# Seven to nine score places between value blocks, and a new order of GpSimd's work, in a fused attention and feed-forward kernel

## The chip, the cores and the metric

The kernel runs on one core of one Trainium2 chip. The metric is the device time of one launch in microseconds; lower is better. TensorE is called PE here as in the profile, VectorE DVE, ScalarE ACT, GpSimd POOL, and SP is the engine whose queue issues the DMAs.

## The reference

```
xn  = layernorm(A_x)                                  # 1 x 2048 x 512
q, k, v = split(xn @ wqkv)                            # 32 heads of 16
p   = softmax(q @ k.T * 16**-0.5)                     # 2048 x 2048 for every head
s   = concat(p @ v) @ wo
h   = (xn @ w_gate) * (xn @ w_up)                     # 2048 x 1792
g   = silu(h @ w_down)
out = A_x + s * g
```

Everything is float32. The projections and feed-forward products are made of three float32r products each (high by high, high by low, low by high), from operands that have been split into a high part and a rest.

## The kernel before

The sequence is cut into 4 chunks of 512 queries and 16 blocks of 128 keys, the heads into 8 groups of 4. A unit `i` is one group and one chunk of queries; there are 32 units, each of 16 *rounds*, one for each block of keys, each of 4 *places*, one for each head: 512 rounds and 2048 places in all.

At a place `expo` issues one matmul `t` (128 keys by 512 queries, line 624, PSUM banks tagged `st`, of which there are three) and ACT's exponential of it into one of 11 `e` buffers (line 626). Beside it, `score` issues a matmul `s` for a unit 21 rounds ahead (line 599, three banks tagged `s`) and DVE's maximum over it (line 601); those maxima become the offsets of the later exponentials. `t` and `s` use different 64-row halves of PE, so they run side by side. The last 21 rounds have no `s`.

Every two rounds `block` (line 629) multiplies their eight `e` tiles with the values: 8 float32 matmuls `pv` in 32-column strips, 16 records in the trace, into one more `st` bank. ACT copies the bank to `part` (line 646) and POOL adds it to the unit's sum `acc` (line 647). Late in the kernel DVE adds it from PSUM itself (line 643). The block of two rounds is issued when four more places have been issued, so twelve places are outstanding for 11 buffers, and the twelfth exponential waits for the block.

The other work of PE is the *filler*: 13 pairs of projections `p`, 56 pairs of gate and up products `g` and `u`, 24 pairs of down products `y`, then the output products `z`. `pair` (line 273) makes two products at once, one on the lower and one on the upper half of PE, in two halves of 12 slots (15 for most `y`). Between the halves ACT reads one element (`look`, line 294), and the second half waits for it. When a pair of projections or of gate and up is done, ACT copies its first product out of PSUM at once, in the place where the filler then stands. DVE's part of it (for `g` and `u` the product, line 354), with the splits on POOL that belong to it, is put in the list `before_values` and issued just before the next block.

`Filler` spreads the filler over cycles, from one block to the next. A first sum gives the number of cycles of each pair, two or three, so that 2328 slots fill 240 cycles; a pair of 24 slots in three cycles has 8, then 7 (4 of the first half and 3 of the second), then 9. In a cycle of eight places the filler stands in the six gaps that `GAPS` names, not behind the first place and not behind the last before the block.

After the 240 cycles `ending` supplies the output products `z`, in pairs of 24 slots over two cycles each, for the first three chunks of queries and, without the last four heads, for the fourth. `end` multiplies with the gate and adds the input. `finish` normalises a unit (two 32 by 32 transposes, a reciprocal and a product). After the last block `finish`, `last_heads` and `final` do this for the last unit and add its product to the fourth chunk's banks.

PE, ACT and DVE run in the order of the program. For POOL and SP that holds for the first 18 rounds only; afterwards the compiler's scheduler orders their queues.

## Time and profile before

| | us |
|---|---|
| median of 3 runs | 1743.56 (1740.57 to 1744.34) |
| the profiled execution | 1742.61 |
| its span, first to last instruction | 1740.8 |
| PE busy | 1720.9 |
| DVE busy | 1453.0 |
| ACT busy | 1324.5 |
| POOL busy | 872.3 |

The mean granted clock of PE was 0.997. In the views that follow, a row of the timeline has the start in us, the duration, engine, line, operation, tiles and count, and in brackets the engine's idle time before it with what ended it. A row of the table by stretch has the stretch, its length and each engine's busy time with its number of instructions, then the granted clock, the share of the DMA engines and GB/s. A row of the waits has the waiting instruction, the one waited for, the total in us, the number of times and the longest.

### The profile page before, as it was taken

Reading aid. Unit: us, or ns where it says so; the run is one execution under the profiler, and the core shown is the slowest. Engines: PE = TensorE matmul, PEld = TensorE weight load, DVE = VectorE, ACT = ScalarE, POOL = GpSimd, SP = SyncE. Lnnn points to the kernel's source line nnn. Section 1 sums busy time; section 2 is a strip of 40 time slices with the busy share of each in tenths; the row PEclk is TensorE's granted clock in tenths of the full one; section 3 lists DMA queues with packets and bytes.
Section 4 is the critical chain, followed back from the end, with each engine's and each line's share of the span. In section 5 each row is a group of like instructions: output and inputs, shape, how many; then the busy total and the mean of one; then the engine's idle time right before and its main releaser. Section 6 shows DMA issues by size and latency. Waiting matters only on the chain.

```text
span 1740.8 us, 35038 instructions
## 1 busy us (share of the span) xinstructions
PE 1720.9 (99%) x13574; PEld 1063.8 (61%) x13574; DVE 1453.0 (83%) x2454; ACT 1324.5 (76%) x2567; POOL 872.3 (50%) x906
## 2 busy tenths in 40 slices
PE   8999999999999999999999999999999999999998
PEld 6666566666666666666666665666666666666654
DVE  6788788888888888888888888888888888888843
ACT  6357778778777778877777888877778777777774
POOL 5225444654654547455364663653547455365450
PEclk9999999999999999999999999999999999999999
DMA  5317533611231132421015220411135121011342
GB/s 206 106 47 223 206 134 117 155 53 35 60 82 49 49 101 78 77 53 54 29 57 125 71 65 29 102 53 41 45 97 123 42 53 53 29 55 50 129 144 73
DMA packets 117234, 145.78 MB, mean 84 GB/s; under 512 B 12620, under 2 KB 74060, under 8 KB 114380
## 3 DMA queue, kind: packets, MB, share of 16 engines
q1 hardware_dynamic: 117068, 143.55, 28.1%
q8 instruction: 106, 1.74, 0.4%
q14 instruction: 60, 0.49, 0.1%
HBM read 95.94 MB, written 47.45 MB: 82 GB/s over the span
## 4 chain that ended last, share of the span: by engine, by line
PE 93%; POOL 2%; DVE 2%; DMA 1%; ACT 1%; issue 1%; SPq 0%; POOLq 0%; ACTq 0%; DVEq 0%
PE pv L637 26%; PE t L624 17%; PE s L599 13%; PE u L286 6%; PE g L286 5%; PE y L290 5%; PE y L286 4%; PE u L290 3%; PE p L286 3%; PE g L290 3%; PE v L267 2%; PE z L286 1%; PE p L290 1%; DVE mx L601 1%; PE z L290 1%
## 5 line engine op out<-in xcount | busy, mean ns | idle before, releaser
L601 DVE TENSOR_REDUCE mx<-s 128x1 f32<-128x512 f32 x2048 | 1273.5, 684 | 219.6 <-PE s L599 178.4
L626 ACT ACTIVATE e<-t 128x512 f32<-128x512 f32 x2048 | 1109.3, 603 | 248.7 <-PE pv L637 198.8
L624 PE MATMUL t<-qs,ks 50*128 50x512 f32 x2048 | 785.0, 408 | 5.5 <-ACT part L646 5.0
L599 PE MATMUL s<-ks,qs 48*128 48x512 f32 x2048 | 782.8, 416 | 0.4 <-DVE mx L601 0.4
L624 PEld LDWEIGHTS t<-qs,ks 50*128 50x128 f32 x2048 | 359.2, 185 | 286.1 <-ACT e L626 217.8
L637 PE MATMUL pv<-e,V 128*32 128x512 f32 x4096 | 492.6, 598 | 0.0
L64 POOL TENSOR_TENSOR acc<-acc,part 128x512 f32<-128x512 f32 x214 | 276.1, 1290 | 398.4 <-ACT part L646 398.0
L599 PEld LDWEIGHTS s<-ks,qs 48*128 48x128 f32 x2048 | 350.1, 184 | 29.7 <-issue 5.0
L637 PEld LDWEIGHTS pv<-e,V 128*32 128x32 f32 x4096 | 107.0, 109 | 234.0 <-issue 197.6
L646 ACT ACTIVATE part<-pv 128x512 f32<-128x512 f32 x214 | 128.2, 599 | 85.0 <-PE pv L637 74.2
L64 POOL CAST w0h<-w0r 128x512 fp32r<-128x512 f32 x60 | 36.7, 611 | 110.3 <-PE g L290 63.9
L286 PE MATMUL u<-fh,w0h 64*128 64x512 f32 x224 | 90.6, 405 | 0.0
L290 PE MATMUL g<-fh,w1h 64*128 64x512 f32 x224 | 90.4, 404 | 0.0
L290 PE MATMUL y<-dh,hh 64*128 64x512 f32 x224 | 89.5, 399 | 0.1
L286 PE MATMUL y<-dh,hh 64*128 64x512 f32 x224 | 89.3, 399 | 0.2 <-DVE y L421 0.2
L286 PE MATMUL u<-fh,w0l 64*128 64x512 f32 x224 | 88.2, 394 | 0.0
L286 PE MATMUL g<-fh,w1l 64*128 64x512 f32 x224 | 88.1, 393 | 0.0
L286 PE MATMUL y<-dl,hh 64*128 64x512 f32 x224 | 88.0, 393 | 0.0
L290 PE MATMUL g<-fl,w1h 64*128 64x512 f32 x224 | 88.0, 393 | 0.0
L290 PE MATMUL g<-fh,w1l 64*128 64x512 f32 x224 | 88.0, 393 | 0.0
L286 PE MATMUL g<-fl,w1h 64*128 64x512 f32 x224 | 88.0, 393 | 0.0
L290 PE MATMUL u<-fl,w0h 64*128 64x512 f32 x224 | 87.9, 392 | 0.0
(258 smaller groups left out, 3034.3 us busy)
## 6 DMA issues: line engine op xcount, KB each, us to landing
w1r<-in_wg_dram SPq DMA_DIRECT2D x56, 256.0 KB
w0r<-in_wu_dram SPq DMA_DIRECT2D x56, 256.0 KB
wdr<-in_wd_dram SPq DMA_DIRECT2D x56, 256.0 KB
qs<-QD SPq DMA_DIRECT2D x64, 192.0 KB
ks<-KD SPq DMA_DIRECT2D x12, 768.0 KB
KD<-hl SPq DMA_DIRECT2D x16, 512.0 KB
QD<-hl SPq DMA_DIRECT2D x16, 512.0 KB
OD<-acc SPq DMA_DIRECT2D x31, 256.0 KB
```

The lines of the kernel that those rows point to most:

```text
L64: got = getattr(self.engine, name)(*args, **kw)
L267: nc.tensor.matmul(o, l(d), r(d), start=k == d == 0, stop=k == 2 and d == ND - 1)
L286: nc.tensor.matmul(outs[k], l[LOWER], r[LOWER], start=k == 0 and n == 0, stop=(stop or k == 0) and n == len(low) - 1, skip_group_check=k == 1)
L290: nc.tensor.matmul(outs[1 - k], l[UPPER], r[UPPER], start=k == 0 and m == 0, stop=(stop or k == 0) and m == len(high) - 1, skip_group_chec ...
L599: nc.tensor.matmul(o, QS[i][b:b + KB, pr, t * P:(t + 1) * P], k[b:b + KB, pr, kc * 512:(kc + 1) * 512], start=True, stop=True)
L601: nc.vector.tensor_reduce(MX[i][:, j, t, kc:kc + 1], o, axis=AX.X, op=OP.max)
L624: nc.tensor.matmul(o, k[b:b + KR, pr, kt * P:(kt + 1) * P], QS[i][b:b + KR, pr], start=True, stop=True)
L626: nc.scalar.activation(e, o, AF.Exp, scale=DH ** -0.5)
L637: nc.tensor.matmul(o[32 * j:32 * j + 32], V[:, kt, h0:h0 + 32], es[j], start=n == 0, stop=n == len(todo) - 1)
L646: nc.scalar.activation(part, o, AF.Copy)
```

## The change

Where a block stands is no longer fixed. For each cycle the new loop asks the filler for the cycle's slots (`begin`), and takes 7, 8 or 9 places by them; the block may stand 1 to 5 places behind the last place of its own two rounds. The filler then spreads its slots over all gaps but the first and the last. The split of `Filler.fetch` into cycles is as before.

`before_values` is joined by `behind_values`, which is run just after the block: the stores of projections and the splits of the gated products move into it, behind the block's sum on POOL. For the first three chunks `end` makes the product on DVE before the block and the addition on POOL behind it, where DVE did both. The first output pair gets three cycles, the others two as before. The last unit's normalisation is done in two halves of 256 queries, with the rest of the split on POOL, and the final matmuls go in pairs of tiles, the first two parts of them among the slots of the last pair. Cut to its core:

```diff
-GAPS = [(0, 1, 2), (1, 2, 3)]
+AHEAD = range(1, 6)
-FINAL_AT = 8
+WITH_LAST = (8, 12)
...
             nc.vector.tensor_copy(raws[1], outs[1])
+            behind_values.append(lambda: store(raws))
+        def store(raws):
             for o, (_, w, c) in zip(raws, which):
...
         nc.vector.tensor_tensor(g, u, g, op=OP.mult)
-        split_rows(g, hi, lo)
+        behind_values.append(lambda: split_rows(g, hi, lo))
 
...
-        if t % 2 or c < NC - 1:
+        if t % 2 and c == NC - 1:
+            if c < NC - 1:
+                behind_values.append(lambda: add(tt, yt, xt))
+                return
+        dma(out[tt * P:(tt + 1) * P], yt)
+    def add(tt, yt, xt):
+        pool.tensor_tensor(yt, yt, xt, op=OP.add)
...
-                    soon(n, lambda u=t + n, o=o, got=got[n]: end(c, u, o, *got))
+                    before_values.append(lambda u=t + n, o=o, got=got[n]: end(c, u, o, *got))
...
-        def final(t):
-            th, tl = fst["t"]
-            sl = slice(t * P, (t + 1) * P)
-            for n, (l, r) in enumerate(((th, wrh), (th, wrl), (tl, wrh))):
-                nc.tensor.matmul(banks[t], l[:, sl], r, start=False, stop=n == 2, skip_group_check=True)
-            end(NC - 1, t, banks[t], fst["y"][:, t], xr[:, t])
-        todo = [0, 1, 2, 3]
-        left = 24
+        def final(todo, kinds):
+            for n in kinds:
+                k, r = ((0, wrh), (0, wrl), (1, wrh))[n]
+                for t in todo:
+                    nc.tensor.matmul(banks[t], fst["t"][k][:, t * P:(t + 1) * P], r, start=False, stop=n == 2,
+                                     skip_group_check=True)
+            if 2 in kinds:
+                for t in todo:
+                    end(NC - 1, t, banks[t], fst["y"][:, t], xr[:, t])
+        late = [((0, 1), (0, 1)), ((0, 1), (2,)), ((2, 3), (0, 1)), ((2, 3), (2,))]
+        count = 0
-            left -= v == 1
-            if "t" in fst and left == FINAL_AT:
-                final(todo.pop(0))
-                final(todo.pop(0))
+            count += v == 1 and "t" in fst
+            if count in WITH_LAST and v == 1:
+                final(*late.pop(0))
-        for t in todo:
-            final(t)
-    def last_heads():
-        fp = fst["fp"]
-        th, tl = [fp.tile([P, 512], F32, name="g", bufs=2).bitcast(F32R) for _ in range(2)]
-        nc.scalar.activation(th, fst["tn"], AF.Copy)
-        nc.vector.tensor_tensor(tl, fst["tn"], th, op=OP.subtract)
-        fst["t"] = th, tl
+        for _ in range(WITH_LAST[0] - count):
+            nc.tensor.matmul(psum("st", "warm"), wrh[:, 0:P], wrh, start=True, stop=True)
+        for part in late:
+            final(*part)
...
                                  start=n == 0, stop=n == len(todo) - 1)
-        if todo[0][1] == 0:
+        if now[0] == NU * NT - 1 and todo[0][1] == NT - 1:
+            last_heads(o)
+        elif todo[0][1] == 0:
             sums[i] = keep.tile([P, 512], F32, name="acc", bufs=2)
...
+    def last_heads(o):
+        i = NU - 1
+        acc = sums.pop(i)
+        tr = keep.tile([P, 16, 32], F32, name="tr", bufs=1)
+        rc = keep.tile([P, 16, 1], F32, name="rc", bufs=1)
+        th, tl = fst["t"] = [fst["fp"].tile([P, 512], F32, name="g", bufs=2).bitcast(F32R) for _ in range(2)]
+        for h in range(2):
+            c, b = slice(256 * h, 256 * h + 256), slice(8 * h, 8 * h + 8)
+            flat = tr[:, b].rearrange("p b e -> p (b e)")
+            nc.vector.tensor_tensor(acc[:, c], o[:, c], acc[:, c], op=OP.add)
+            nc.vector.transpose(flat, acc[:, c])
+            nc.vector.reciprocal(rc[:, b], tr[:, b, DH:DH + 1])
+            nc.vector.tensor_tensor(tr[:, b, 0:DH], tr[:, b, 0:DH], rc[:, b].to_broadcast([P, 8, DH]), op=OP.mult)
+            nc.vector.transpose(acc[:, c], flat)
+            nc.scalar.activation(th[:, c], acc[:, c], AF.Copy)
+            pool.tensor_tensor(tl[:, c], acc[:, c], th[:, c], op=OP.subtract)
     def run(gen):
...
-                    first = n - self.split
-                    self.plan = self.share(first, 6 * self.whole) if self.whole else []
+                    self.more = max(2, self.split - 1) if odd and self.whole else n if odd else 0
+                    self.queue = self.share(n - self.split, self.whole) if self.whole else []
-                        self.plan += self.share(self.split, 2)
-                else:
-                    self.plan = []
-                    if self.split:
-                        more = max(2, self.split - 1) if self.whole else n
-                        self.plan = [0] + self.share(more, 3)
-                        n -= more
+                        self.queue.append((self.split, self.more))
-                        self.plan += self.share(n, 6 * self.whole)
-        def part(self, first=True):
-            if first and not self.left and not self.done:
+                        self.queue += self.share(n - self.more, self.whole)
+        def begin(self):
+            if not self.left and not self.done:
-            if self.left:
-                n = min(self.left, self.plan.pop(0) if self.plan else self.left)
-                for _ in range(n):
-                    next(self.gen)
-                self.left -= n
+            self.now = self.queue.pop(0) if self.left and self.queue else self.left
+            both = self.now if isinstance(self.now, tuple) else (self.now,)
+            return sum(both)
+        def spread(self, gaps):
+            if isinstance(self.now, tuple):
+                a, b = self.now
+                self.plan = self.share(a, 2) + [0] + self.share(b, gaps - 3)
+            else:
+                self.plan = self.share(self.now, gaps)
+        def part(self):
+            n = self.plan.pop(0) if self.plan else 0
+            while n and self.left:
+                next(self.gen)
+                n -= 1
+                self.left -= 1
...
-    prev = []
-    def values():
+    def values(rounds):
         if before_values:
-            run_ahead()
+            run_all(before_values)
         else:
             step_small(heads)
-        block(prev)
-        if prev[-1][1] == NT - 1:
-            heads.append(finish(prev[0][0]))
+        block(rounds)
+        run_all(behind_values)
+        if rounds[-1][1] == NT - 1:
+            heads.append(finish(rounds[0][0]))
             step_small(heads)
-        prev.clear()
+    ready = {}
+    def position(q):
+        n, j = divmod(q, 4)
+        i, kt = divmod(n, NT)
+        g, c = divmod(i, NC)
+        now[0] = n
+        Tied.on = n < 18
+        if j == 0:
+            if kt == 8 and i + 2 < NU:
+                load_q(i + 2)
+            if kt == 0 and g + 1 < NG and c == 1:
+                load_k(g + 1)
+            ready[n] = i, kt, []
+        if j == 3 and kt % 4 == 2:
+            step_small(later)
+        ready[n][2].append(expo(i, kt, j))
+        si, sr = divmod(n + LEAD, NT)
+        if si < NU:
+            score(si, sr, j ^ 1)
+        step()
+        if j == 1:
+            prepare()
+        if j == 3 and sr == NT - 1 and si < NU:
+            maxima(si, 8 if si < NU - 1 else 4)
+    TOTAL = NU * NT * 4
 
     with tc.manual_schedule(engines=ORDERED):
         with banks_of(EARLY_BUFS):
             fil = Filler(filler(early()), spread)
         ctx.enter_context(banks_of(BUFS))
-        for n in range(NU * 16):
-            now[0] = n
-            Tied.on = n < 18
-            i, kt = divmod(n, 16)
-            g, c = divmod(i, NC)
-            si, sr = divmod(n + LEAD, 16)
-            if kt == 8 and i + 2 < NU:
-                load_q(i + 2)
-            if kt == 0 and g + 1 < NG and c == 1:
-                load_k(g + 1)
-            es = []
-            if n == 0:
-                run(fst["v"])
-            for j in range(4):
-                if j == 3 and kt % 4 == 2:
-                    step_small(later)
-                es.append(expo(i, kt, j))
-                if si < NU:
-                    score(si, sr, j ^ 1)
-                step()
-                if j == 1:
-                    prepare()
-                if n and j in GAPS[n % 2]:
-                    if fil.done:
-                        fil = Filler(ending(), lambda n: 2)
-                    fil.part(n % 2 and j == 1)
-            if sr == 15 and si < NU:
-                maxima(si, 8 if si < NU - 1 else 4)
-            if n and n % 2 == 0 or n == NU * 16 - 1:
-                values()
-            prev.append((i, kt, es))
-        run_ahead()
-        block(prev)
-        run(finish(NU - 1))
+        run(fst["v"])
+        q = 0
+        while q < 4:
+            position(q)
+            q += 1
+        for b in range(NU * NT // 2):
+            if fil.done:
+                parts = iter([3] + [2] * 8)
+                fil = Filler(ending(), lambda n: next(parts))
+            work = fil.begin()
+            if b >= NU * NT // 2 - 2:
+                last = TOTAL - 4 * (NU * NT // 2 - 1 - b)
+            else:
+                fits = min(9, max(7, int(2.5 + 0.62 * work))) if q + 4 * LEAD < TOTAL and work else 8
+                need = 8 * (b + 1)
+                last = min(max(q + fits, need + AHEAD[0]), need + AHEAD[-1], TOTAL - 4)
+            count = last - q
+            fil.spread(max(3, count - 2))
+            for k in range(count):
+                position(q)
+                q += 1
+                if 0 < k < count - 1 or count < 3:
+                    fil.part()
+            if b < NU * NT // 2 - 1:
+                values([ready.pop(2 * b), ready.pop(2 * b + 1)])
+        values([ready.pop(NU * NT - 2)])
+        run_all(before_values)
+        run_all(behind_values)
+        block([ready.pop(NU * NT - 1)])
         flush()
-        last_heads()
         while fil.left or not fil.done:
             now[0] += 1
             prepare()
-            fil.part()
+            if not fil.left:
+                fil.fetch()
+            for _ in range(fil.left):
+                next(fil.gen)
+            fil.left = 0
+            fil.fetch()
             flush()
     ffp.close()
 
```

More of the change, by code (lines that the diff above doesn't have):

```diff
@@ L138, in step, with run_all @@
             waiting.pop(0)[1]()
-    before_values = []
-    def run_ahead():
-        while before_values:
-            before_values.pop(0)()
+    before_values, behind_values = [], []
+    def run_all(queue):
+        while queue:
+            queue.pop(0)()
     ep = ctx.enter_context(tc.tile_pool(name="ep", bufs=1))
@@ L814, in __init__ @@
             self.gen, self.cycles = gen, cycles
-            self.left, self.plan, self.done = 0, [], False
+            self.left, self.queue, self.done = 0, [], False
+            self.plan = []
         def share(self, n, gaps):
@@ L910, in body @@
-        run_ahead()
-        block(prev)
-        run(finish(NU - 1))
+        run(fst["v"])
[23 more added lines that the diff above has]
+                values([ready.pop(2 * b), ready.pop(2 * b + 1)])
@@ L913, in body @@
+        values([ready.pop(NU * NT - 2)])
+        run_all(before_values)
+        run_all(behind_values)
+        block([ready.pop(NU * NT - 1)])
         flush()
-        last_heads()
         while fil.left or not fil.done:
```

14 lines of the change are left out of this document (6 added, 8 removed).

## The prediction

> **What bounds the kernel now.** I read the page's busy times and chain, then the table of time by stretch for one repeat of the schedule, then the timeline around a value block. A cycle here runs from the start of one value block to the next; a slot is two half-height matmuls side by side (a `t` with an `s`, or a low with a high feed-forward half).
>
> ```profile
> PE 1720.9 (99%) x13574; PEld 1063.8 (61%) x13574; DVE 1453.0 (83%) x2454; ACT 1324.5 (76%) x2567; POOL 872.3 (50%) x906
> PE 93%; POOL 2%; DVE 2%; DMA 1%; ACT 1%; issue 1%; SPq 0%; POOLq 0%; ACTq 0%; DVEq 0%
> ```
>
> PE carries 93% of the chain, so the question is which cycles hold PE up. These are the five cycles of two feed-forward pairs, all engines first, then line 286 alone, whose count is the slots of filler:
>
> ```profile
> 789.65:796.37 6.72, 6.72 (x59) 4.19 (x57) 6.16 (x11) 5.69 (x12) 6.18 (x7) 1.00 0.28 78
> 803.12:809.12 6.00, 6.00 (x51) 3.73 (x49) 5.05 (x10) 5.01 (x10) 5.92 (x7) 1.00 0.33 88
> 809.12:815.10 5.98, 5.98 (x48) 3.52 (x47) 4.87 (x9) 4.61 (x11) 1.74 (x2) 1.00 0.20 53
> 815.10:821.12 6.02, 6.02 (x51) 3.70 (x50) 4.92 (x10) 4.60 (x10) 1.85 (x3) 1.00 0.09 22
> sum 31.47, PE 31.47 PEld 19.59 DVE 26.48 ACT 24.96 POOL 17.58; mean PE 6.29 PEld 3.92 DVE 5.30 ACT 4.99 POOL 3.52
> 789.65:796.37 6.72, 3.76 (x12) 2.25 (x12) 1.00 0.28 78
> 803.12:809.12 6.00, 2.83 (x8) 1.50 (x8) 1.00 0.33 88
> 809.12:815.10 5.98, 2.55 (x7) 1.31 (x7) 1.00 0.20 53
> 815.10:821.12 6.02, 3.05 (x9) 1.69 (x9) 1.00 0.09 22
> ```
>
> From 9 to 12 slots of filler the time rises (6.72 - 6.02)/3 = 0.233 us a slot: PE is the bound. A cycle with 8 score places and w slots then wants 6.72 - 0.233 (12 - w): 5.79 for w = 8 and 5.555 for w = 7. Both take 5.98 to 6.00, so something else sets a floor; 0.2 and 0.43 us are lost there.
>
> ```profile
> ACT e L626 <- PE pv L637: 198.8, 248, 1.3
> 809.12 1.92 PE L637 MATMUL pv<-e,V 128*32 128x512 f32 x16
> 810.20 0.60 ACT L626 ACTIVATE e<-t 128x512 f32<-128x512 f32 x1 [1.00 <-PE pv L637]
> 811.17 0.60 ACT L646 ACTIVATE part<-pv 128x512 f32<-128x512 f32 x1 [0.37 <-PE pv L637]
> 811.66 1.57 ACT L626 ACTIVATE e<-t 128x512 f32<-128x512 f32 x3
> 811.32 0.39 PE L624 MATMUL t<-qs,ks 50*128 50x512 f32 x1
> 811.82 0.18 PEld L624 LDWEIGHTS t<-qs,ks 50*128 50x128 f32 x1
> 812.02 0.40 PE L624 MATMUL t<-qs,ks 50*128 50x512 f32 x1
> 813.31 0.50 PE L286 MATMUL u<-fh,w0h 64*128 64x512 f32 x1
> 813.65 0.39 PE L624 MATMUL t<-qs,ks 50*128 50x512 f32 x1
> 811.54 4.88 DVE L601 TENSOR_REDUCE mx<-s 128x1 f32<-128x512 f32 x8 [1.11 <-PE s L599]
> ```
>
> The floor is VectorE's: maxima start 2.42 us into the cycle and follow every (4.88 - 0.69)/7 = 0.60. With three `s` banks the eighth `s` waits for the fifth maximum, 2.42 + 4 x 0.60 + 0.69 = 5.51, and the block follows 0.47 later: 5.98. With seven places the same sum gives 2.42 + 1.80 + 0.69 + 0.47 = 5.38.
>
> The rows give four more prices, from the block's start. The buffer of a *blocked* exponential (11 `e` buffers; the twelfth outstanding place must wait for the block) is free at 1.08. ScalarE operations follow each other every (1.57 - 0.60)/2 = 0.49. A `t` whose bank comes free at 811.17 + 0.60 = 811.77 has its matmul at 812.02, 0.25 later. After an exposed wait the next slot takes 0.34 instead of 0.233 (813.31 to 813.65). The second `t` of a cycle starts at 2.20.
>
> **Places between blocks.** The rule is 7 places for w = 7 or 8, 8 for w = 9 or 10, 9 for w = 11 or 12, held between 1 and 5 places past the block's own rounds (now always 4). Applied to the 240 filler cycles it closes after five: 9, 9, 7, 7, 8 for w = 12, 12, 8, 7, 9, with 4, 5, 4, 3, 3 ahead. The number of slots doesn't change, so cycles where PE is the bound only trade time (0.233 a place), and the floor is the prize.
>
> Counted out: 74 cycles (12 filler, 9 places) and nine (11, 9) gain a place: 83 x 0.233 = +19.3 us. The 41 cycles (7, 7) want 5.32 of PE and 5.38 of VectorE; the pause for ScalarE's `look` adds some: I take 5.45 (5.32 to 5.56), 41 x (5.45 - 5.98) = -21.7. The (9, 8) cycles stay. There are 41 cycles (8, 7), and their price depends on how many places were ahead when they began.
>
> Eight begin with at most 4 ahead: 5.56 against 6.00, -3.5. The other 33 begin with 5, that is with *two* blocked exponentials, which hold the next two `t` banks. Behind one block the second runs at 1.08 + 0.49 = 1.57 and ends at 2.17; its bank serves the second `t` at 2.42 instead of 2.20, and with the slow step after it the cycle is 5.555 + 0.22 + 0.11 = 5.88. Seven follow a `y` pair and are such: -0.8.
>
> In the other 26 a pair of projections or of gate and up has just ended, and its ScalarE copy is queued between them. Before, it ran ahead of the only blocked one:
>
> ```profile
> 802.99 0.60 ACT L398 ACTIVATE g<-g 128x512 f32<-128x512 f32 x1
> 804.00 0.65 DVE L354 TENSOR_TENSOR g<-u,g 128x512 f32<-128x512 f32 x1
> 804.20 0.60 ACT L626 ACTIVATE e<-t 128x512 f32<-128x512 f32 x1 [0.61 <-PE pv L637]
> ```
>
> The copy is issued after the last filler slot, one place before the block. With 5 ahead that place's exponential is already blocked, so the order becomes exponential 1.08, copy 1.57, exponential 2.06 to 2.66, part copy 2.55. The second `t` comes at 2.91: 0.71 late, and PE takes matmuls in order, so the `s`, the fillers and six more places queue behind it. 5.555 + 0.71 + 0.11 = 6.37 against 6.00: 26 x 0.37 = +9.6. The product on VectorE waits for the copy too (2.2 to 2.9), and the filler's first bank with it, no later than PE gets there.
>
> [...]
>
> Eighteen further cycles keep 5 ahead and begin without a copy (0.33 each, +5.9), four with one (0.82, +3.3). Together: 19.3 - 21.7 - 3.5 - 0.8 + 9.6 + 5.9 + 3.3 = **+12.1 us**.
>
> **GpSimd's order.** Splits and stores go behind the block's sum.
>
> ```profile
> ACT part L646 <- POOL acc L64: 6.4, 2, 4.5
> PE t L624 <- ACT part L646: 5.0, 2, 3.7
> 184.48:195.61 11.13, 7.39 (x48) 3.82 (x47) 6.31 (x12) 4.97 (x11) 7.49 (x8) 0.85 0.65 227
> 341.97:349.29 7.32, 6.10 (x50) 3.20 (x48) 5.50 (x12) 4.76 (x10) 7.16 (x9) 1.00 0.25 72
> ```
>
> Only twice did the sum come too late for the part copy: cycles of 11.13 and 7.32 where 5.98 and 6.00 are usual, 6.5 us together. Both should go: **-6.5** (bounds -6.5 and +4: a store that leaves GpSimd later also holds the weight loads behind it in SP's queue, and a new late sum is possible). The split that now waits behind the sum is not needed until the last `y` slots, a cycle later.
>
> **The end.** The first output pair gets three cycles instead of two, so 12 slots (2.8 us) leave the cycles and pass to the end of the queue. End products give up their second VectorE pass.
>
> ```profile
> PEld z L290 <- DVE hh L464: 2.7, 3, 1.2
> 1725.22:1740.84 15.62, 8.40 (x41) 4.74 (x40) 8.25 (x13) 1.00 (x2) 2.55 (x2) 0.82 0.18 67
> 1727.24 0.69 DVE L643 TENSOR_TENSOR acc<-pv,acc 128x512 f32<-128x512 f32 x1 [0.19 <-PE pv L637]
> 1730.20 0.63 ACT L555 ACTIVATE g<-acc 128x512 fp32r<-128x512 f32 x1 [4.62 <-DVE acc L664]
> 1730.89 0.50 PE L536 MATMUL z<-hl,g 128*128 128x512 f32 x1 [2.14 <-ACT g L555]
> 1732.00:1735.00 3.00, 3.00 (x8) 2.34 (x8) 2.04 (x4) 0.00 (x0) 1.28 (x1) 0.50 0.00 0
> 1736.60 0.69 DVE L464 TENSOR_TENSOR y<-z,hh 128x512 f32<-128x512 f32 x1
> ```
>
> The waits for those products go: -2.7. The last short cycle takes a few slots more (+0.6), and ten cycles without scores start with 5 ahead (0.2 each, +2). After the last block four slots of the last pair's first half remain, then `look`, then 12 slots and 12 final matmuls. `look` stands behind both halves' copies on ScalarE. The heads' chain took 1730.20 - 1727.24 = 2.96 before its copy; two halves one after the other take about as long, so `look` comes near 1.92 + 0.1 + 3.0 + 0.5 = 5.5 and PE idles from 2.20 + 3 x 0.233 = 2.9. 24 slots bring PE to 5.6 + 24 x 0.233 = 11.2. The rows show the granted clock at 0.50 for 3 us after PE's 2.14 us of idleness, which would cost 1.5 again: 12.7, then 1.4 to 2 for the last tile, 14.4 against 1737.29 - 1725.22 = 12.07: +2.3. Sum of the end -2.8 - 2.7 + 0.6 + 2.0 + 2.3 = **-0.6** (-6 to +5).
>
> [...]
>
> **Sum.** +12.1 - 6.5 - 0.6 = +5.0 on a profiled 1742.6 (span 1740.8 and 1.8 around it), which lies 0.95 under the median 1743.6. On the median: 1748.6, said as **1749**. This kernel's runs spread over 0.2% (3.5 us), about what a measurement can tell from no change.
>
> **Rivals.** *Balanced as the rule means it:* two blocked exponentials don't hold PE, because banks or buffers come free sooner than the rows suggest. All 33 cycles (8, 7) then run at 5.56 and the 22 others pay nothing: +19.3 - 21.7 - 41 x 0.44 = -20.4; with -7.1 from the rest, 1716. For it: the losses at the floor are real. Against: in 248 of the 256 cycles a blocked exponential does wait for the block. 0.16. *Only the copy is early:* the second exponential holds PE by 0.33, but the copy costs nothing: 1749 - 30 x 0.49 = 1734. For it: the copy's input is ready long before. Against: its place in the queue. 0.13. *GpSimd doesn't obey:* its queue is ordered by the scheduler once the first rounds are over, so the two stalls stay, or move to another block: 1755. For it: one such stall held PE for 3.7 us. 0.19. The forecast keeps 0.52.
>
> **Numbers.** The range takes half of the fast rival out below and the obstinate GpSimd in above: 1729 to 1759. Faster by over 0.2%: 0.16 + 0.11 = 0.27; within: 0.02 + 0.18 of the forecast's lower side = 0.20; slower 0.53.
>
> **What would show it.** Cycles with 7 places near 5.45 (w = 7) and 6.37 (w = 8), 9 places near 6.95; in the slow ones two exponentials with a `g` between them after the block, and the second `t` 2.9 us in, waiting for ScalarE. No wait of `part` on the sum. A `look` after the heads' copies with PE idle before it. Cycles (8, 7) at 5.6 would prove the main step wrong.

## The result, and the profile after

The changed kernel takes 1764.06 us (median of 4 runs, 1757.47 to 1765.33) against 1743.12 for the kernel before beside it; by the means of the runs it is 1.0114 times as long, with a 95% interval of 1.0087 to 1.0142. The forecast of 1749 had the direction and was 15 us short; the range ended at 1759. The profiled execution took 1765.33, its span 1763.5 against 1740.8: 22.7 us to account for.

From the page after, engine busy times and the chain by engine:

```profile
PE 1728.2 (98%) x13574; PEld 1057.2 (60%) x13574; DVE 1434.4 (81%) x2446; ACT 1309.8 (74%) x2568; POOL 886.7 (50%) x920
PE 88%; POOL 3%; ACT 3%; DMA 2%; issue 2%; DVE 1%; SPq 0%; POOLq 0%; ACTq 0%
```

PE's busy time rose by 7 us only, and its share of the chain fell from 93% to 88%: the chain now runs through ACT, POOL and DMAs at places where PE waits. The table by stretch shows one repeat of five cycles, places 9, 9, 7, 7, 8:

```profile
899.92:906.89 6.97, 6.97 (x60) 4.34 (x58) 6.42 (x12) 5.83 (x12) 6.18 (x7) 1.00 0.27 78
906.89:913.86 6.97, 6.97 (x61) 4.39 (x59) 5.85 (x12) 5.12 (x11) 2.10 (x4) 1.00 0.00 0
913.86:920.03 6.17, 5.82 (x48) 3.28 (x46) 5.02 (x10) 5.00 (x10) 6.12 (x7) 1.00 0.33 90
920.03:925.58 5.55, 5.55 (x46) 3.01 (x44) 4.11 (x8) 4.19 (x10) 1.29 (x1) 1.00 0.27 55
925.58:931.62 6.04, 6.04 (x52) 3.71 (x51) 4.76 (x9) 4.71 (x10) 1.86 (x3) 1.00 1.07 163
sum 31.70, PE 31.34 PEld 18.73 DVE 26.17 ACT 24.84 POOL 17.55; mean PE 6.27 PEld 3.75 DVE 5.23 ACT 4.97 POOL 3.51
```

Before, the five took 31.47. The two long cycles gained 0.25 each, the short one with 7 slots lost 0.43, and the middle one, with 7 places and 8 slots, went from 6.00 to 6.17, where the forecast had 6.37. In it alone PE isn't busy throughout (5.82 of 6.17).

To set the whole span out in the same way, I call a *stall* what a cycle takes over the median of the cycles with its places and slots, where that is over 0.25 us. Up to the start of cycle 239 the rest of the cycles, summed by class, is the steady part; from there on it is the end.

| us | before | after | measured | forecast |
|---|---|---|---|---|
| steady cycles | 1506.2 | 1511.9 | +5.7 | +12.1 |
| stalls | 9.4 | 22.3 | +12.9 | -6.5 |
| the end | 117.4 | 121.5 | +4.1 | -0.6 |

The largest stalls before are cycle 12 (5.15), 36 (1.33), 237 (1.05) and 8 (0.96), of six; after, cycle 36 (5.95), 8 (4.20), 237 (3.47), 137 (1.20) and 12 (1.09), of 21. So the term that failed most is the one called "GpSimd's order".

### The profile page after: what moved, and what is told of

It reads as the page before. It is cut to its first block, busy times and chain, and to the rows that moved or that the text cites. A ratio compares the mean times of both kernels' runs of the same rounds, so it can differ in the third digit from the quotient of the medians.

```text
span 1763.5 us, 35082 instructions
## 1 busy us (share of the span) xinstructions
PE 1728.2 (98%) x13574; PEld 1057.2 (60%) x13574; DVE 1434.4 (81%) x2446; ACT 1309.8 (74%) x2568; POOL 886.7 (50%) x920
## 4 chain that ended last, share of the span: by engine, by line
PE 88%; POOL 3%; ACT 3%; DMA 2%; issue 2%; DVE 1%; SPq 0%; POOLq 0%; ACTq 0%
PE pv L643 24%; PE t L630 18%; PE s L605 11%; PE u L286 5%; PE g L286 5%; PE y L286 5%; PE y L290 4%; PE u L290 3%; PE g L290 3%; PE v L267 2%; PE p L290 2%; PE p L286 2%; PE z L286 2%; DMA wdr<-in_wd_dram 1%; ACT e L632 1%
## 5 line engine op out<-in xcount | busy, mean ns | idle before, releaser
L630 PE MATMUL t<-qs,ks 50*128 50x512 f32 x2048 | 800.2, 412 | 17.2 <-ACT e L632 11.4
L630 PEld LDWEIGHTS t<-qs,ks 50*128 50x128 f32 x2048 | 366.3, 186 | 299.7 <-ACT e L632 174.4
L605 PEld LDWEIGHTS s<-ks,qs 48*128 48x128 f32 x2048 | 356.2, 185 | 35.5 <-DVE mx L607 8.9
L286 PE MATMUL u<-fh,w0h 64*128 64x512 f32 x224 | 90.6, 404 | 0.0
L290 PE MATMUL g<-fh,w1h 64*128 64x512 f32 x224 | 90.3, 403 | 0.0
L290 PE MATMUL u<-fh,w0h 64*128 64x512 f32 x224 | 88.7, 396 | 0.0
L286 PE MATMUL g<-fl,w1h 64*128 64x512 f32 x224 | 88.3, 394 | 0.0
L286 PE MATMUL g<-fh,w1l 64*128 64x512 f32 x224 | 88.3, 394 | 0.0
L286 PE MATMUL g<-fh,w1h 64*128 64x512 f32 x224 | 88.2, 394 | 0.0
```

Of the source, the lines that this page charges most:

```text
L286: nc.tensor.matmul(outs[k], l[LOWER], r[LOWER], start=k == 0 and n == 0, stop=(stop or k == 0) and n == len(low) - 1, skip_group_check=k == 1)
L290: nc.tensor.matmul(outs[1 - k], l[UPPER], r[UPPER], start=k == 0 and m == 0, stop=(stop or k == 0) and m == len(high) - 1, skip_group_chec ...
L605: nc.tensor.matmul(o, QS[i][b:b + KB, pr, t * P:(t + 1) * P], k[b:b + KB, pr, kc * 512:(kc + 1) * 512], start=True, stop=True)
L630: nc.tensor.matmul(o, k[b:b + KR, pr, kt * P:(kt + 1) * P], QS[i][b:b + KR, pr], start=True, stop=True)
```

## The experiments

**Which part of the change costs.** Four kernels, each with one part undone. In the first two the multiplication, addition and store of token tiles 10 and 11 are left out, since the deferred queue is not run again behind the last block.

`fixed_eight`: eight places in every cycle, four ahead; lists and end are those of the changed kernel.

```diff
-AHEAD = range(1, 6)
+AHEAD = range(4, 5)
-                fits = min(9, max(7, int(2.5 + 0.62 * work))) if ... else 8
+                fits = 8
```

> The changed kernel with its places fixed again at eight, always four ahead; GpSimd's new order and the new end stay. In the two profiles the ordinary cycles grew by 5.8 us, the cycles far above their kind's median by 12.9 us, and the stretch from the last filler cycle on by 4.1 us. Theory A (the stalls belong to the order of GpSimd's and SP's queues, whatever the places): the ordinary cycles return to the times of before, 5.98 and 6.73, the stalls stay near 22 us in sum, total about 1759. Rival B (the stalls come of the moved places): stalls near 9 us, total about 1746.

Measured: 1742.03, 0.9995 of before (0.9986 to 1.0005). Theory B. Its steady part is 1506.6 and its stalls add up to 9.7 us with 5.05 in cycle 12, as before. So ahead of cycle 239, where nothing is left out, the new order of the lists is worth nothing that can be told, and the loss there comes with the places. What the new end is worth this kernel doesn't show: what it leaves out lies there, and the same omission makes 6.4 us between `ahead_four` and `four_whole` below.

`ahead_four`: 7 to 9 places, but at most four ahead.

```diff
-AHEAD = range(1, 6)
+AHEAD = range(1, 5)
```

> The changed kernel with the block held 1 to 4 places ahead instead of 1 to 5, so that at most one exponential is blocked. Theory A (the second blocked exponential, with the copy queued between the two, holds PE): cycles of 7 places and 8 slots fall from 6.18 to about 5.56 in all 41, the cycles of 8 places and 12 slots that began with five ahead from 6.89 and 7.34 to 6.73; together some 20 us off, total about 1743. Rival B (a cycle with 7 places has a floor of its own near 6.2, from ScalarE or VectorE): no cycle gets faster, total 1764.

Measured: 1735.93, 0.9962 (0.9947 to 0.9977). Beyond theory A. The 41 cycles of 7 places and 8 pairs, but for cycle 36 with its stall, fell to a mean of 5.585, the steady part to 1494.0, which is 12.2 under before; the stalls were 16.6. In the profiles the fifth place ahead costs 23.7 us ahead of cycle 239, where nothing is left out, 18.0 of them in the steady part. The whole difference of 28 us has the work that is left out in it as well.

`splits_in_front`: the deferred splits and stores issued ahead of the block again.

```diff
-        block(rounds)
         run_all(behind_values)
+        block(rounds)
```

> The changed kernel with the stores and splits issued in front of the block again; places and end stay. Theory A (the stalls come of the new order of GpSimd's and SP's queues): the sum of the excess over the median of each kind of cycle falls from 22 us to about 9, total about 1751. Rival B (the stalls come of the moved places): total about 1764, excess near 22. Rival C (the prediction's own step, the new order takes stalls away): total about 1771.

Measured: 1764.68, 1.0130 (1.0113 to 1.0147). Theory B: stalls 23.0 us, cycle 36 4.74, cycle 8 4.73, cycle 237 4.04. Where the program puts the sum is not what makes the stalls.

`end_in_twos`: the first output pair in two cycles, as before.

```diff
-                parts = iter([3] + [2] * 8)
+                parts = iter([2] * 9)
```

> The changed kernel with two cycles for the first output pair, as for all others, so that the last pair's first half is over before the last block. Theory A (the element that ScalarE reads between the halves stands behind the last heads' copies, PE idles 3.4 us and its clock falls): that wait goes, the stretch behind the last block falls from 21.9 to about 14, while 12 more slots lie in the cycles before (2.8 us): total about 1759. Rival B (the chain of the last heads sets the tail, whatever stands between): the stretch stays above 18 and the total at 1764.

Measured: 1770.02, 1.0158 (1.0143 to 1.0173): slower, against both theories. Its last stretch is 21.85 us, as in the changed kernel, but cycle 243 has no filler at all, and cycles 244 and 245 take 7.59 and 10.75 (6.14 and 8.01 in the changed kernel). So three cycles for the first pair cost less than two.

**The cycle of 7 places and 8 pairs.** ACT's timeline for such a cycle in the changed kernel, whose block starts at 913.86, then PE's:

```profile
914.94 0.60 ACT L632 ACTIVATE e<-t 128x512 f32<-128x512 f32 x1 [1.56 <-PE pv L643]
915.43 0.59 ACT L401 ACTIVATE g<-g 128x512 f32<-128x512 f32 x1
915.91 0.60 ACT L632 ACTIVATE e<-t 128x512 f32<-128x512 f32 x1
916.39 0.62 ACT L654 ACTIVATE part<-pv 128x512 f32<-128x512 f32 x1
```
```profile
915.71 0.50 PE L630 MATMUL t<-qs,ks 50*128 50x512 f32 x1
916.57 0.50 PE L630 MATMUL t<-qs,ks 50*128 50x512 f32 x1 [0.35 <-ACT e L632]
```

That is the order of the forecast: exponential at 1.08 into the cycle, copy at 1.57, exponential at 2.05, part copy at 2.53. The second `t` comes 2.71 in. The 26 cycles with this order take 6.16 to 6.21, but for cycle 36 with its stall. The seven that begin five ahead without a copy take 5.71 to 5.84, the eight with at most four ahead 5.55 to 5.58. `early_copy` moves the copy and leaves everything else: the filler of a nine-place cycle is shared over one gap fewer.

```diff
-            fil.spread(max(3, count - 2))
+            fil.spread(max(3, count - 2 - (count == 9)))
```

> The kernel after, with the feed-forward products of a nine-place cycle shared over one gap fewer, so that the pair's copy on ScalarE is queued ahead of the next cycle's two blocked exponentials instead of between them. Theory A (the copy between them is what the five places ahead cost): the 26 cycles of seven places and sixteen products that take 6.16 to 6.21 us fall to about 5.75, what the seven such cycles without a copy take, which is -11 us; the stall of cycle 8, which begins with that copy, loses 2 us: 1751. Theory B (the fifth place ahead costs by itself): they stay at 6.18, the time at 1764. Theory C: the gap without products ahead of the value block leaves TensorE waiting in the 73 long cycles, 0.1 us each: 1771.

Measured: 1752.09, 1.0056 (1.0039 to 1.0072), 12.0 under the changed kernel. The same cycle, whose block starts at 906.28 here, ACT and then PE:

```profile
905.96 0.60 ACT L401 ACTIVATE g<-g 128x512 f32<-128x512 f32 x1
907.37 1.08 ACT L632 ACTIVATE e<-t 128x512 f32<-128x512 f32 x2 [0.81 <-PE pv L643]
```
```profile
908.14 0.49 PE L630 MATMUL t<-qs,ks 50*128 50x512 f32 x1
908.50 0.49 PE L630 MATMUL t<-qs,ks 50*128 50x512 f32 x1
```

The copy stands ahead of the block, the second `t` comes 2.22 in, and the cycle takes 5.68 instead of 6.17. Theory A, shown: of the 26, 19 fell to 5.67 to 5.76, and six that follow a cycle of eight places, which this edit doesn't touch, keep the copy between the exponentials and take 6.18 to 6.20 still; the last one is cycle 36. The long cycles did not lengthen, so theory C falls.

The stall of cycle 8 went from 4.20 to 1.53 with it, as theory A said. In the changed kernel the late copy held up stores, and behind them in SP's queue a weight load, whose split then stood ahead of the sum in POOL's (waits from 145 to 170 us):

```profile
POOL w1h L64 <- DMA w1r<-in_wqkv_dram: 2.3, 1, 2.3
DVE tr L666 <- POOL acc L64: 3.2, 1, 3.2
```

The two waits are 1.2 and 2.1 in `early_copy`, whose POOL and SP have the same order up to there. But cycle 12 went from 1.09 to 4.55, and the stalls add up to 22.8 us against 22.3 in the changed kernel: the 12 us gained are the steady part, which fell by 13.3.

**The stalls.** How far one profile of a stall can be trusted is seen where two kernels differ only at the end. The changed kernel, `gpsimd_copies` and `end_in_twos` have the same order of instructions on POOL and on SP up to cycle 235, and their cycle 36 is 5.95, 4.67 and 3.95 over; `ahead_four`, `four_whole` and `four_filled` below share another order, and theirs is 2.41, 4.98 and 4.26. A difference of 2.5 us in one stall can be chance.

Around cycle 36 the waits of POOL and of those who wait for it, window 310 to 362 us, in the changed kernel and before:

```profile
POOL dh L64 <- DMA wdr<-in_wd_dram: 10.8, 3, 9.3
ACT part L654 <- POOL acc L64: 3.8, 1, 3.8
PE t L630 <- ACT part L654: 3.4, 1, 3.4
```
```profile
POOL dh L64 <- DMA wdr<-in_wd_dram: 8.0, 3, 4.4
ACT part L646 <- POOL acc L64: 1.9, 1, 1.9
PE t L624 <- ACT part L646: 1.2, 1, 1.2
```

The chain is the same and longer. SP's timeline tells why the load came later, the changed kernel first, then before:

```profile
319.13 1.83 SPq L64 DMA_DIRECT2D ks<-KD  x1
321.78 10.35 SPq L64 DMA_DIRECT2D wdr<-in_wd_dram  x3
```
```profile
319.78 0.84 SPq L64 DMA_DIRECT2D wdr<-in_wd_dram  x2
320.67 0.43 SPq L64 DMA_DIRECT2D ks<-KD  x1
```

The load of the keys, 768 KB, overtook the first two loads of `wdr`, 256 KB each. POOL then did in turn what had gathered (changed kernel, its timeline):

```profile
329.79 0.61 POOL L64 CAST dh<-wdr 128x512 fp32r<-128x512 f32 x1 [9.28 <-DMA wdr<-in_wd_dram]
...
346.58 1.26 POOL L64 TENSOR_TENSOR hl<-g,hh 128x512 fp32r<-128x512 f32 x1
347.80 2.61 POOL L64 TENSOR_TENSOR acc<-acc,part 128x512 f32<-128x512 f32 x2
```

The next part copy waits for the first of the two sums at 347.80, in a cycle that began at 342.61 and took 12.12. Its row in the table by stretch:

```profile
342.61:354.73 12.12, 8.37 (x48) 4.63 (x46) 5.96 (x11) 5.45 (x10) 11.96 (x15) 0.76 0.28 80
```

PE's idle time there is 12.12 - 8.37 = 3.75, and the stall is 5.95: the rest is the granted clock of 0.76. If the clock is 1 or one half, as the rows of 1 us in the last section read except where it changes, 2 x 0.24 x 12.12 = 5.8 us of the cycle ran at half. The other long stalls of the changed kernel are made of the same two parts, a wait of 2.21 and a clock of 0.83 in cycle 8, 1.66 and 0.90 in cycle 237; before, only cycle 12 was (3.74 and 0.85). Four kernels tested the waits.

`five_from_forty`: four ahead in the first 40 cycles, five from there on.

```diff
-                last = min(max(q + fits, need + AHEAD[0]), need + AHEAD[-1], TOTAL - 4)
+                last = min(max(q + fits, need + AHEAD[0]), need + (4 if b < 40 else 5), TOTAL - 4)
```

> The kernel after, held to four places ahead in the first 40 cycles and to five from there on. Theory A (the stalls of cycles 8 and 36 come from the fifth place): they fall from 4.2 and 5.95 us to about 2.0 and 2.4, as with four ahead throughout, and the eight cycles of seven places and sixteen products there go from 6.18 to 5.57 us, -4.9: 1753. Theory B (the stalls belong to cycles of seven and nine places, however far ahead they begin): only the -4.9, 1759.

Measured: 1757.31, 1.0087 (1.0069 to 1.0104), between the theories. In the profile, which is of the slowest of its four runs (1762.39), cycles 8 and 36 fell to 2.36 and 3.0, but cycle 12 rose to 5.08 (1.09) and cycle 237 to 5.58 (3.47). What was gained at 8 and 36 came back there, in cycle 237 perhaps by chance. No theory of mine said that.

`tied_eighty`: POOL and SP held to the program's order for 80 rounds.

```diff
-        Tied.on = n < 18
+        Tied.on = n < 80
```

> The kernel after, with GpSimd's and SyncE's instructions held to the program's order for 80 rounds (40 cycles) instead of 18, so that in cycles 32 to 36 the loads of the down-projection's weights (wdr) stand ahead of the 768 KB load of the keys in SyncE's queue, and a sum ahead of all splits behind it. Theory A (the stall of cycle 36 is that load's place in the queue): 5.95 us fall to at most 1.5, 1759.5. Theory B (GpSimd is simply full in cycles 34 to 36, whatever it waits for): the stall stays at 4 to 6 us, 1764. Theory C (the program's order holds loads behind stores that are not ready): new stalls between cycles 9 and 40, 1766 to 1775.

Measured: 1776.95, 1.0195 (1.0181 to 1.0209). Cycles 12 and 36 no longer stall at all, as theory A has it, and cycle 8 keeps its 4.36. But cycles 33, 38 and 30 now take 6.72, 7.28 and 3.54 too long. Theory C, and dearer than I thought. Two stretches of it and the waits in 325 to 378 us:

```profile
325.56:338.36 12.80, 8.34 (x53) 5.05 (x51) 6.00 (x11) 4.79 (x10) 7.35 (x8) 0.73 0.33 104
364.04:377.40 13.36, 7.55 (x53) 4.39 (x51) 5.77 (x10) 5.18 (x11) 9.24 (x12) 0.80 0.32 91
```
```profile
PE t L630 <- DMA qs<-MD: 5.8, 1, 5.8
DVE acc L673 <- POOL tr L64: 5.7, 1, 5.7
```

In place of the sum, the offsets of the exponentials (`qs<-MD`) and a unit's normalisation are late. That each stands in one of the two queues behind something that isn't ready is the likely reason; it wasn't tried.

`no_wdr_wait`: the splits of the first five down-projection blocks read a tile that is there already; the loads stay, and those blocks' weights are left out of the products.

```diff
+                    if c == ti == 0:
+                        raw = V[:, i, 0:512]
                     soon(8, lambda raw=raw, i=i, dh=dh, dl=dl: split_rows(raw, dh[:, i], dl[:, i]))
```

> The kernel after, where the splits of the first five down-projection blocks of chunk 0 read a tile that has long been in SBUF (the values) instead of the freshly loaded wdr, whose loads are still issued; those five blocks' weights are so left out of the computation. Theory A (the stall of cycle 36 is GpSimd's 9.3 us wait for wdr): it falls from 5.95 to at most 1.5 us, 1759.5. Theory B (GpSimd has too much queued in cycles 34 to 37 by itself): 4 us or more remain, 1763.

Measured: 1758.90, 1.0094 (1.0078 to 1.0110), 5.2 under the changed kernel. Cycle 36 takes 6.18, the usual time: its stall is gone whole, and no wait of `part` for the sum is left in that window. Theory A: POOL isn't overfull there, it lost 9 us to a load.

`maxima_on_vector`: the small subtraction of the maxima on DVE.

```diff
-        (pool if i < NU - 1 else nc.vector).tensor_tensor(mm[:, :, 1], m, mm[:, :, 0], op=OP.subtract)
+        nc.vector.tensor_tensor(mm[:, :, 1], m, mm[:, :, 0], op=OP.subtract)
```

> The kernel after, with the subtraction of the maxima (mm, 32 times, 128x16) on VectorE instead of GpSimd. Theory A (cycle 237 stalls since that subtraction stands behind GpSimd's sum and splits): its 3.47 us fall to about 1, the stalls of other cycles stay, VectorE's 32 small operations lie in its idle time: 1761.5. Theory B (cycle 237 waits for something else, the unit's last sum among others): 3 us or more remain, 1764.

Measured: 1768.69, 1.0149 (1.0133 to 1.0165). In the changed kernel that subtraction stood in POOL's queue behind splits and a sum, and DVE waited for it in cycle 237:

```profile
DVE mt L618 <- POOL mm L64: 2.6, 1, 2.6
```

Cycle 237 went from 10.45 to 7.19: so far theory A. Its price was misjudged: cycles all through the kernel in which a unit's maxima end became up to 1.0 us longer, and the first line (this kernel) stands against the second (changed kernel) in the waits of the whole span:

```profile
PEld s L605 <- DVE mx L607: 13.8, 23, 2.8
```
```profile
PEld s L605 <- DVE mx L607: 8.9, 12, 2.6
```

**The end.** The changed kernel's timeline behind the last block (ACT, then PE) and the granted clock by stretch:

```profile
1747.51 0.42 ACT L693 ACTIVATE g<-acc 128x256 fp32r<-128x256 f32 x1 [1.47 <-DVE acc L692]
1747.83 0.14 ACT L294 ACTIVATE look<-z 1x1 f32<-1x1 f32 x1
1748.03 0.50 PE L286 MATMUL z<-fh,w0h 64*128 64x512 f32 x1 [3.35 <-ACT look L294]
```
```profile
1748.00:1755.00 7.00, 6.97 (x19) 0.53 0.00 0
1755.00:1756.00 1.00, 1.00 (x10) 0.89 0.00 0
```

`look` comes 6.21 after the block's start, behind the second copy, PE has then waited 3.35, and works at half clock for about 7 us. The length of that is partly chance: seven more of these kernels have the same wait of 3.34 or 3.35, and while two (`end_in_twos`, `five_from_forty`) have the clock at half for 6.8 us and a last stretch of 21.9, five (`early_copy`, `splits_in_front`, `tied_eighty`, `no_wdr_wait`, `maxima_on_vector`) have 3.4 and 20.4. `gpsimd_copies` takes the two copies off ACT.

```diff
-            nc.scalar.activation(th[:, c], acc[:, c], AF.Copy)
+            pool.tensor_copy(th[:, c], acc[:, c])
```

> The kernel after, with the two rounding copies of the last heads on GpSimd instead of ScalarE, so that the small `look` copy of the last output pair no longer stands behind them. Theory A (look behind the copies starves TensorE for 3.35 us and the idle time halves its clock): look goes right after the first half of the pair, TensorE waits about 1 us at most, the clock stays near 1.0, the last stretch falls from 21.9 to about 16.5 us and the time to 1759. Theory B (the halved clock comes from the wait for the last heads themselves, whichever engine copies): the longer chain on GpSimd (two copies and two subtractions, some 0.5 and 0.73 us each) keeps TensorE idle over 2 us, the clock is halved all the same, 1764 to 1766.

Measured: 1759.24, 1.0091 (1.0076 to 1.0106): theory A to the microsecond, in part by luck. ACT and PE there, and the last stretch of this kernel:

```profile
1744.62 0.16 ACT L294 ACTIVATE look<-z 1x1 f32<-1x1 f32 x1 [2.35 <-PE z L290]
1744.84 0.50 PE L286 MATMUL z<-fh,w0h 64*128 64x512 f32 x1 [0.25 <-ACT look L294]
```
```profile
1741.53:1757.63 16.10, 9.95 (x58) 5.22 (x57) 8.25 (x17) 0.76 (x2) 4.84 (x6) 0.95 0.22 81
```

PE waits 0.25 instead of 3.35, and the stretch takes 16.1 instead of 21.9 (20.4 in the five) with the same 41 matmuls behind the block. Cycle 245 took back 1.6 of that (9.59 instead of 8.01), and the stalls, in the same order of both queues, happened to be 1.8 less.

**A faster version.** `four_whole` is `ahead_four` with nothing left out.

```diff
             fil.left = 0
+            run_all(before_values)
+            run_all(behind_values)
             fil.fetch()
```

> Four places ahead at most, as in ahead_four, with the queues of deferred work also run behind the last value block: in ahead_four the multiplication, addition and store of token tiles 10 and 11 stood in a queue that nothing ran any more and were left out; here they are done. Theory A (the time of ahead_four is that of its order, not of the work left out): two multiplications, two additions on GpSimd and two stores lie beside the last products, +1 us: 1737. Theory B (GpSimd's two additions and the stores lie on the way to the end): +3 to +5 us, 1740.

Measured: 1742.65, 0.9994 (0.9982 to 1.0006), single runs from 1736.45 to 1746.40. Theory B, though by another way: the deferred multiplications stand behind the last heads on DVE, and the next pair's banks wait for them.

```profile
PE z L286 <- DVE dl L469: 3.4, 1, 3.4
```

PE's clock halves again (0.50 for about 3.4 us), and from cycle 239 on it takes 121.2 us against 114.8 in `ahead_four`. The rest of the difference in the profiles is chance: in the same order of all queues, cycle 36 had PE wait 2.15 and 2.51 us, but was 2.41 over in `ahead_four` at full clock and 4.98 in `four_whole` with the clock halved.

`four_filled` mends the end of `four_whole`: copies on POOL as in `gpsimd_copies`, and an output chunk may begin a round earlier, so that no cycle is without filler.

```diff
-SPLIT_ROUNDS = 4
+SPLIT_ROUNDS = 3
```

> Four places ahead at most, with three ends of the program changed: the deferred queues are also run behind the last value block (nothing is left out), the last heads' rounding copies are on GpSimd, and an output chunk may begin three rounds after its heads' splits instead of four, so that no cycle of the end is without products. Theory A (ahead_four's cycles with the last stretch of gpsimd_copies): from cycle 239 on about 115 us instead of 121.2 in four_whole, 1737, a little faster than before. Theory B (with three rounds TensorE waits for the splits of the heads): a wait of 2 to 4 us at that place, 1741. The stalls of cycles 8, 12, 36 and 237 differ by 5 us between runs of one order, so 1734 to 1742 agrees with A.

Measured: 1733.15, 0.9944 (0.9930 to 0.9958), some 10 us under the kernel before and 31 under the changed one. From cycle 239 on it takes 113.1 where theory A had 115; the stalls are 19.9 still, and the steady part is 1494.0.

`four_filled_tied` adds the 80 rounds of program order.

> The kernel four_filled with the program's order for GpSimd and SyncE held for 80 rounds instead of 18, the edit of tied_eighty. Theory A: the stalls of cycles 12 and 36 (4.9 and 2.4 to 5.0 us with four ahead) fall to about 1 each, 6 us less than four_filled, 1731. Theory B: GpSimd is full there, the same as four_filled, 1737. Theory C: loads held behind stores cost 3 us or more, 1740.

Measured: 1744.34, 1.0010 (1.0001 to 1.0018). Theory C: cycles 12 and 36 are mended, cycles 33 and 38 stall by 9.08 and 6.52.

`four_filled_vector` adds the subtraction on DVE.

> The kernel four_filled with the subtraction of the maxima on VectorE. Theory A: cycle 237's 3.27 us fall to 1, 1731. Theory B: nothing falls, and VectorE pays for 32 operations on its way, 1733 to 1735.

Measured: 1746.20, 1.0016 (1.0008 to 1.0025). Slower than either theory: cycle 237 is mended, but 31 cycles are late by over 0.25 us where 17 were, most of them where a unit's maxima end.

## Why the prediction was right or wrong

**Steady cycles, +12.1 forecast, +5.7 measured: the mechanism was right, one size was not.** The places came as counted, 9, 9, 7, 7, 8, and the cycles of 7 places and 7 slots take 5.55 (5.45 forecast): -18.9 against -21.7. The 41 cycles of 7 places and 8 slots gave 0 instead of +5.3. Their three kinds were as said, 8, 7 and 26, at 5.56, about 5.75 and 6.18; the term mis-sized is the late copy, at 6.37. The forecast let a `t` begin 0.25 after its bank's exponential ended; here it began at 916.57 when that ended at 916.51, 0.06 later. That alone is 0.19 x 26 = 4.9 us. The 0.25 was misread: from 811.54 to 812.02 PE had other matmuls to do without a gap, so that `t` stood behind them and wasn't waiting for its bank. The other cycles, the 82 of nine places among them, cost 24.6 (1039.9 against 1015.3) where 28.5 was forecast. In this trace ACT kept its order: the copy began at 915.43, behind the exponential at 914.94, though the last matmul of its input ended at 913.69 and ACT stood idle for 1.56 us before that exponential. The rival "only the copy is early" priced that at 30 x 0.49 = 14.7; `early_copy` makes it 12.0.

**GpSimd's order, -6.5 forecast, +12.9 measured: this step failed.** It took two stalls for the work of POOL's order within a cycle, and let both go. `fixed_eight` shows that the new order by itself takes none of them away, and `splits_in_front` that taking it back brings none. In the changed kernel cycle 36 is a chain through two queues whose order the scheduler makes, and which differs between the two kernels: a large load ahead of a weight load in SP's queue, then a split that waits for that load ahead of the sum in POOL's. Cycle 8 is one of the same kind, with a store ahead of the load. The places moved, with them the due times, and both queues were filled another way. Of the 13.6 us in cycles 36, 8 and 237, one cause each is shown: `no_wdr_wait` takes cycle 36's 5.95 away, `early_copy` 2.7 of cycle 8's 4.20 (1.2 of them wait, the rest because the clock stayed full), `maxima_on_vector` the 3.47 of cycle 237. The size has a second part that the forecast didn't look at, though its row for the stall of 11.13 shows a clock of 0.85: PE waited for 7.6 of these 13.6 us, and worked 10.6 us of the same three cycles at half clock, which makes 5.3 more. The upper bound of +4 named the first cause ("holds the weight loads behind it in SP's queue") but had one new late sum in mind, not three stalls. The rival "GpSimd doesn't obey" had the mechanism, but priced it at the old stalls.

**The end, -0.6 forecast, +4.1 measured.** The cycles before the last block gave -2.2 (-2.9 forecast). What failed is the stretch behind it, +6.3 where +2.3 was forecast: `look` at 6.21 where 5.5 was forecast, PE idle for 3.35 where 2.6 was, and then the clock at half for about 7 us where the forecast took over the 3 us that followed the idle 2.14 before. The last tile's multiplication ends 18.0 us after the block's start instead of 14.4: 0.7 from `look`, 1.9 from the longer time at half clock ((6.8 - 3) / 2), and 1 that isn't accounted for. Where the half clock lasts 3.4, as in five of the eight kernels with this wait, the stretch is still 20.4. Waits of 2.14 us before and of 3.35 here were both followed by half clock, so taking its cost over from the row of before was right in kind, but too short.

**Luck.** The 0.53 on slower was borne out, but only in part for the reasons given: the steady cycles cost less than half of what was forecast, and 12.9 of the 22.7 us came from the term that was to bring 6.5. The range was too narrow above because the stalls' term was bounded by those seen before, not by how many cycles could get one.

**Still open:** what makes the scheduler choose as it does, and so what would keep all stalls small at once. For cycle 12 (1.09 in the changed kernel, 5.08 in `five_from_forty`) the traces show what comes and goes. In the kernels where it stalls by 4.5 to 5.2, POOL begins the sum 4.1 to 4.8 us into the cycle, behind the splits of two weights and of both projections. In the changed kernel the splits of the weights are done when the cycle begins, one step of the second projection's stands behind the sum, and the sum begins at 1.8.

## What to carry to other kernels

A block moved by one place may change which instruction is last in a queue in order: before letting an engine run one step further ahead, look at what stands between the two waiting instructions on the engine that they share. Where some queues are ordered by a scheduler, the stalls of single steps don't belong to one line of the program; a change of pace can deal them anew, so put several microseconds for them, in both directions, into a forecast, and don't take a stall's size in one profile for its price. And a tiny instruction that another engine waits for is better not issued behind a chain's copies: here that cost 4 to 6 us.

## What the runs showed of the hardware

Behind waits of 2.14 us (before) and 3.44 us (`four_whole`) near the end PE's clock stayed at half for about 3.4 us, behind 3.35 us in the changed kernel for about 6.8. PE's granted clock by stretch, before and then `four_whole`:

```profile
1731.00:1732.00 1.00, 1.00 (x3) 0.88 0.00 0
1732.00:1733.00 1.00, 1.00 (x4) 0.50 0.00 0
...
1734.00:1735.00 1.00, 1.00 (x4) 0.50 0.00 0
1735.00:1736.00 1.00, 0.76 (x3) 0.91 0.76 283
```
```profile
1728.00:1729.00 1.00, 1.00 (x7) 0.88 0.00 0
1729.00:1731.00 2.00, 2.00 (x10) 0.50 0.22 85
1731.00:1732.00 1.00, 1.00 (x3) 0.50 0.46 170
1732.00:1733.00 1.00, 1.00 (x6) 0.91 0.49 184
```

If the clock is 1 or one half, as the rows between these read, a mean of 0.88 is 0.24 us at half: 0.24 + 3.0 + 0.18 = 3.4 us in the first of them, the same in the second, and 2 x 0.47 x 7.0 + 0.22 = 6.8 in the changed kernel, by the two rows shown above. In the changed kernel PE was busy nearly throughout (6.97 of 7.00 us) and the clock stayed low all the same.

Neither whether the clock fell nor how long it stayed low followed from the length of the wait alone. Counted in the same way from the mean clock, 0.79 over 8 us each (2 x 0.21 x 8), it was at half for 3.4 us behind waits of 3.74 us (cycle 12 before), 2.21 and 1.66 (cycles 8 and 237 of the changed kernel); by 0.66 over 10 us (2 x 0.34 x 10) it was at half for 6.8 behind the 3.40 of the changed kernel's cycle 36. A wait of 1.22 us in cycle 36 before left it at 1.00, and the 2.15 in cycle 36 of `ahead_four`, longer than the 1.66 above, left it full as well (the cycle is 2.41 over in all). Why three of the eight kernels with the same wait before the last stretch had 6.8 us at half and the other five 3.4, though PE worked throughout, stays open.
